# Two chunks of 256 tokens at once in the first layer behind the attention

## The chip, the cores and the metric

The kernel runs on one core of one Trainium2 chip. A core has a matrix engine (TensorE, PE in the profile, with its weight loads shown as PEld), VectorE (DVE), ScalarE (ACT), GpSimd (POOL) and SyncE (SP), which here issues all DMAs. Products go to eight PSUM banks of 2 KB for each of 128 partitions; everything else lies in SBUF. The metric is the device time of one execution in microseconds, as a median over several runs.

## The reference

An attention with a memory term feeds two feed-forward layers. All inputs are float32.

```
x = g * (phi(q) @ M_prev) / (phi(q) . z_prev) + (1 - g) * softmax(causal(q k^T / 8)) @ v   # 4 x 8 heads, 576 tokens, 64 wide
x = x as 2304 tokens x 512
h = x @ moe_w_in;   a = 0 where h <= -1, h where h >= 1, (h + 1)^2 / 4 between;   x = a @ moe_w_out
h = x @ moe2_w_in;  a = max(0.01 h, h);                                          out = a @ moe2_w_out
```

The weights are 512 x 2048 and 2048 x 512, and come as 64-bit floats that the kernel decodes itself.

## The kernel before

**Tiling.** The 2304 tokens are nine chunks of 256 (`TC`), held transposed: 128 partitions by four blocks of model width by 256 tokens. The 2048 hidden units are two halves (segments) of eight slots of 128. The first layer runs over the nine chunks with the first half, then over the nine chunks with the second, so it has eighteen numbered chunks, 0 to 17; the second layer has eighteen more, 18 to 35. A chunk of the first layer is eight steps, one for each slot.

**One step.** Each operand is split into a high and a low float32r part, and a product is high x high + high x low + low x high. `mm_h` (L551) makes 12 products of 256 columns into one bank (four blocks of model width, three each). ScalarE passes twice over the result (L565, L566), VectorE takes the minimum with the third form (L567), makes the high part (L569, a cast) and the low part (L571, a subtraction). Two steps later `mm_y` (L575) uses them in 12 products of 256 columns that accumulate, over the eight steps, into two banks: four output blocks of 256 columns, two in a bank. `finish` (L586) empties the two banks. In the first half ScalarE copies the sums (L593) and SP stores them to DRAM; in the second half VectorE adds what was stored before, brought back by `load_prev` (L540), and SP stores the result (L595, L597).

**Banks.** There are five banks called A, two called y and one called h. Behind the attention, the first products of a step take a bank A in turn, and the sums of even chunks go to the two y, those of odd chunks to h and one A (L716). So a chunk's sums and the next chunk's are in different banks.

**What sets the order.** Up to chunk 5 the first layer is woven into the attention, and a scheduler may move instructions. Behind it (L823) TensorE, ScalarE, VectorE and GpSimd run in the order in which the code is written; SP's queue is still placed by the scheduler. Beside the steps stand jobs, given by step number: fetching and decoding weight halves from 64-bit form (L118 to L135, five VectorE instructions and one of ScalarE) and splitting them into high and low parts (L200, L204). Their VectorE instructions are put between those of a step by `fill` (L194): before the cast, before the low part, and behind it. The load of the next chunk's x is issued in step 3, and its split (`high_x` on ScalarE, `low_x` on VectorE) in step 5.

**Buffers.** Tiles live in pools. The attention's pool is closed when the first weights of the second half need room, and a second pool opens over it. `g`, the high and the low part have two buffers each: the high part of step f is written where that of step f - 2 was, when its second products are done.

Of the kernel before, what the change touches and what calls it, by code (L numbers as in the profile page):

```python
# [20 lines left out]
TC = 256  # L21
# [9 lines left out]
again = {n for n, (s, c) in enumerate(CHUNKS) if any(SEGS[t][0] == SEGS[s][0] and d == c for t, d in CHUNKS[:n])}  # L31
NW, RAWB, SPB, EB, GB = 4, 3, 2, (2, 2, 2, 2, 1), 2
# [19 lines left out]
def attn_moe_moe_kernel(ctx, tc, q, k, v, m_prev, z_prev, beta, w1i, w1o, w2i, w2o, out):  # L52
# [92 lines left out]

    def load_raw(seg, f, x):
# [78 lines left out]
    def split_out(seg, p):  # L225


        if (seg, p) not in combos:
            combine(seg, p)
        b11, t1, b, t = combos.pop((seg, p))  # L230
        wa = wts.tile([128, 2, 512], F32R, tag=f"o{2 * p}", name="wa")
        wb = wts.tile([128, 2, 512], F32R, tag=f"o{2 * p + 1}", name="wb")
        ex = l2_pool().tile([128, 2, 768], F32R, tag=f"ex{p}", name="ex")
# [277 lines left out]
    def load_x(n):  # L511
        seg, c = CHUNKS[n]
        layer = SEGS[seg][0]
        xf = ffn.tile([128, 4, TC], F32, tag="xf", bufs=1, name="xf")
# [25 lines left out]
    def load_prev(n):  # L540

        seg, c = CHUNKS[n]
        if SEGS[seg][0] == 0:
            pp = ffn.tile([128, 1024], F32, tag="xf", bufs=1, name="xf")
        else:
            pp = l2_pool().tile([128, 1024], F32, tag="pp", name="pp")
# [4 lines left out]
    def mm_h(n, f):  # L551
        seg, c = CHUNKS[n]
        w = slots[f, 0]
        xh, xl = xin[n]
        hp = psum()[:, 0:TC] if attended else ps.tile([128, TC], F32, tag="h", bufs=HB, name="h")
        for ct in range(4):
            wh, wl = w[:, 0, 128 * ct:128 * ct + 128], w[:, 1, 128 * ct:128 * ct + 128]
            nc.tensor.matmul(hp, wh, xh[:, ct], start=(ct == 0), stop=False)  # L558
            nc.tensor.matmul(hp, wh, xl[:, ct], start=False, stop=False)  # L559
            nc.tensor.matmul(hp, wl, xh[:, ct], start=False, stop=(ct == 3))  # L560
        g = ffn.tile([128, TC], F32, tag="g", bufs=2, name="g")
        gh = ffn.tile([128, TC], F32R, tag="gh", bufs=GB, name="gh")
        gl = ffn.tile([128, TC], F32R, tag="gl", bufs=GB, name="gl")
# [4 lines left out]
        fill()  # L568
        nc.vector.tensor_copy(gh, g)  # L569
        fill()  # L570
        nc.vector.tensor_tensor(gl, g, as_r(gh), ALU.subtract)  # L571
        fill()
        return gh, gl

    def mm_y(n, f, yp, gg):  # L575
        w = slots[f, 1]
        gh, gl = gg
        for et in range(4):
            wh, wl = w[:, 0, 128 * et:128 * et + 128], w[:, 1, 128 * et:128 * et + 128]
            o = yp[et // 2][:, et % 2]  # L580

            nc.tensor.matmul(o, wh, gh, start=(f == 0 and et % 2 == 0), stop=False)  # L582
            nc.tensor.matmul(o, wh, gl, start=False, stop=False)  # L583
            nc.tensor.matmul(o, wl, gh, start=False, stop=(f == NSLOT - 1 and et % 2 == 1))  # L584

    def finish(n, yp):  # L586
        c = CHUNKS[n][1]
        pp = prev.pop(n, None)
        for i in range(2):
# [7 lines left out]
            nc.sync.dma_start(out=dst, in_=ys.rearrange("p (b t) -> p b t", b=2))  # L597


    def mm_h2(n, p):  # L600
# [12 lines left out]
        g = l2_pool().tile([128, 8, 128], F32, tag="g2", bufs=2, name="g2")  # L613
# [6 lines left out]
        gh = l2_pool().tile([128, 7, 128], F32R, tag="gh2", bufs=2, name="gh2")  # L620
        gl = l2_pool().tile([128, 7, 128], F32R, tag="gl2", bufs=2, name="gl2")
# [14 lines left out]
    def finish2(n, yp):  # L636
        seg, c = CHUNKS[n]
        pp = prev.pop(n, None)
        s0 = l2_pool().tile([128, 2, 256], F32, tag="s0", name="s0")
        s1 = l2_pool().tile([128, 2, 256], F32, tag="s1", name="s1")  # L640
# [41 lines left out]
    for seg in range(1, N1):  # L682
        x0 = START[seg]
        order = sorted((x0 + f + (-7, -5)[x], f, x) for f in range(NSLOT) for x in range(2))
# [27 lines left out]
    def layer1_y():  # L712
        nonlocal yp
        n, f, gg = pend.pop(0)
        if f == 0:
            yp = [bank(t) for t in ("h" + "Ah"[HB - 1] if attended and n % 2 else "yy")]  # L716
        mm_y(n, f, yp, gg)
        if f == NSLOT - 1:
            finish(n, yp)

    def layer1_steps():
        load_x(0)
        low_x(0, high_x(0))
        for n, (seg, c) in enumerate(CHUNKS):
            if SEGS[seg][0] == 1:
                break
            for f in range(NSLOT):
                do_jobs(8 * n + f)
                pend.append((n, f, mm_h(n, f)))
                if f == (3 if attended else 5):  # L730
                    load_x(n + 1)
                if f == 5:
                    low_x(n + 1, high_x(n + 1))
                if f == 6 and n in again:
                    load_prev(n)
# [118 lines left out]
```

## Time and profile before

| | |
|---|---|
| median of 3 runs | 1116.9 us (1115.13 to 1118.41) |
| the profiled execution | 1113.12 us, span of the trace 1111.3 us |
| TensorE busy | 1060.2 us, 8520 products |
| VectorE, ScalarE busy | 851.4 us, 612.4 us |
| mean granted TensorE clock | 0.98 of full speed |

The profile is one execution. A busy time is the union of an engine's instructions; products are pipelined, so their mean length (283 ns for 256 columns) is longer than the distance between their starts, and the distance is what counts. The time before an instruction in which its engine was idle is listed with what released it. The attention fills the first 430 us together with chunks 0 to 5 of the first layer; chunks 6 to 17 lie between 432 and 715 us, and the second layer behind them.

### The profile page before, as it was taken

To read this page: it belongs to the slowest core of one execution; us is meant where nothing else is said; L and a number is where in the kernel's file an instruction comes from. 1 tells how busy PE (TensorE), PEld (TensorE's weight loads), DVE (VectorE), ACT (ScalarE), POOL (GpSimd) and SP (SyncE) were. 2 spreads that over 40 slices of the span, in tenths; PEclk is the share of its full clock that TensorE was granted. 3 is DMA by queue.
4 is the path that set the end of the run, shared out by engine and by line. 5 is a ranking of instruction groups with operands and counts; after the bars stand their busy time and mean duration, and the time that the engine had idled before them with its cause. 6 is when DMAs were issued, how large, how long until landed. Compare 5 with 4: busy or idle time off the path is not lost.

```text
span 1111.3 us, 22273 instructions
## 1 busy us (share of the span) xinstructions
PE 1060.2 (95%) x8520; PEld 1002.1 (90%) x8520; DVE 851.4 (77%) x2244; ACT 612.4 (55%) x1379; POOL 28.9 (3%) x28
## 2 busy tenths in 40 slices
PE   5877899999999999999999999999999999999997
PEld 4655777888889889999999999999999999999997
DVE  6698899876777666985776777898887899657655
ACT  6898787666666664464333334554444465334332
POOL 0000000000000000000000000000000001112111
PEclk9888999999999999999999999999999999999999
DMA  6465545442334223531343333223222111311311
GB/s 145 115 166 150 161 129 160 121 117 68 88 79 120 65 58 93 168 100 56 96 152 115 116 117 121 86 77 133 95 96 96 58 39 49 104 58 65 103 44 58
DMA packets 122170, 112.08 MB, mean 101 GB/s; under 512 B 67280, under 2 KB 100048, under 8 KB 122064
## 3 DMA queue, kind: packets, MB, share of 16 engines
q1 hardware_dynamic: 122064, 110.66, 33.8%
q8 instruction: 67, 1.10, 0.4%
q14 instruction: 39, 0.32, 0.1%
HBM read 77.60 MB, written 23.59 MB: 91 GB/s over the span
## 4 chain that ended last, share of the span: by engine, by line
PE 81%; DVE 9%; DMA 4%; ACT 3%; issue 1%; SPq 1%; DVEq 0%; ACTq 0%
PE A L612 6%; PE A L611 6%; PE A L610 6%; PE A L558 4%; PE A L560 4%; PE A L559 4%; PE y L582 4%; PE y L583 4%; PE y L584 4%; PE y L634 3%; PE y L633 3%; PE y L632 3%; PE A L371 3%; PE A L423 2%; PE h L558 2%; PE h L559 2%
## 5 line engine op out<-in xcount | busy, mean ns | idle before, releaser
L612 PE MATMUL A<-xh,i 128*128 128x256 f32 x576 | 163.1, 283 | 0.1
L610 PE MATMUL A<-xh,i 128*128 128x256 f32 x576 | 163.0, 283 | 0.0
L611 PE MATMUL A<-xl,i 128*128 128x256 f32 x576 | 163.0, 283 | 0.0
L772 ACT ACTIVATE gh<-g 128x896 fp32r<-128x896 f32 x72 | 68.8, 955 | 125.0 <-PE A L633 74.2
L565 ACT ACTIVATE g<-A 128x256 f32<-128x256 f32 x98 | 37.6, 384 | 150.9 <-PE A L560 149.7
L751 DVE TENSOR_TENSOR gl<-g,gh 128x896 fp32r<-128x896 f32 x72 | 86.7, 1204 | 33.7 <-ACT gh L772 33.7
L558 PE MATMUL A<-xh,i 128*128 128x256 f32 x392 | 111.0, 283 | 0.0
L559 PE MATMUL A<-xl,i 128*128 128x256 f32 x392 | 110.9, 283 | 0.0
L560 PE MATMUL A<-xh,i 128*128 128x256 f32 x392 | 110.9, 283 | 0.0
L612 PEld LDWEIGHTS A<-xh,i 128*128 128x128 f32 x576 | 110.6, 192 | 0.3 <-DVE i L206 0.3
L610 PEld LDWEIGHTS A<-xh,i 128*128 128x128 f32 x576 | 110.6, 192 | 0.0
L611 PEld LDWEIGHTS A<-xl,i 128*128 128x128 f32 x576 | 110.6, 192 | 0.0
L583 PE MATMUL y<-gl,o 128*128 128x256 f32 x384 | 109.4, 288 | 0.0
L582 PE MATMUL y<-gh,o 128*128 128x256 f32 x384 | 107.4, 291 | 1.6 <-ACT ys L593 1.4
L584 PE MATMUL y<-gh,o 128*128 128x256 f32 x384 | 108.5, 285 | 0.0
L386 ACT ACTIVATE e<-e,mx 128x128 f32<-128x128 f32 (+2 forms) x144 | 84.2, 587 | 20.9 <-DVE mx L383 20.7
L383 DVE CUSTOM_DVE_ANT_0 e<-A,mask 128x384 f32<-128x384 f32 (+4 forms) x126 | 60.2, 481 | 45.0 <-PE A L371 43.8
L615 ACT ACTIVATE g<-A 128x512 f32<-128x512 f32 x72 | 42.8, 594 | 88.8 <-PE A L612 88.8
L567 DVE SCALAR_TENSOR_TENSOR g<-A,g 128x256 f32<-128x256 f32 x98 | 41.3, 422 | 55.6 <-ACT g L566 55.0
L558 PEld LDWEIGHTS A<-xh,i 128*128 128x128 f32 x392 | 75.2, 192 | 0.4 <-issue 0.4
L560 PEld LDWEIGHTS A<-xh,i 128*128 128x128 f32 x392 | 75.3, 192 | 0.0
L559 PEld LDWEIGHTS A<-xl,i 128*128 128x128 f32 x392 | 75.3, 192 | 0.0
(252 smaller groups left out, 3350.3 us busy)
## 6 DMA issues: line engine op xcount, KB each, us to landing
raw<-in_moe_w_in_dram SPq DMA_DIRECT2D x32, 512.0 KB, 3.8
raw<-in_moe_w_out_dram SPq DMA_DIRECT2D x32, 512.0 KB, 3.4
qk<-qk SPq DMA_DIRECT2D x64, 144.0 KB, 2.6
xf<-y_d SPq DMA_DIRECT2D x18, 512.0 KB, 4.2
xf<-x_d SPq DMA_DIRECT2D x12, 512.0 KB, 4.2
yp_d<-ys SPq DMA_DIRECT2D x18, 256.0 KB, 2.2
xf<-yp_d SPq DMA_DIRECT2D x9, 512.0 KB, 3.3
y_d<-ys SPq DMA_DIRECT2D x18, 256.0 KB, 2.2
```

The lines of the kernel that those rows point to most:

```text
L386: nc.scalar.activation(e[:, 0:w], e[:, 0:w], AF.Exp, bias=mx, scale=-1.0, accum_out=ls[:, h:h + 1])
L558: nc.tensor.matmul(hp, wh, xh[:, ct], start=(ct == 0), stop=False)
L559: nc.tensor.matmul(hp, wh, xl[:, ct], start=False, stop=False)
L560: nc.tensor.matmul(hp, wl, xh[:, ct], start=False, stop=(ct == 3))
L582: nc.tensor.matmul(o, wh, gh, start=(f == 0 and et % 2 == 0), stop=False)
L583: nc.tensor.matmul(o, wh, gl, start=False, stop=False)
L584: nc.tensor.matmul(o, wl, gh, start=False, stop=(f == NSLOT - 1 and et % 2 == 1))
L610: nc.tensor.matmul(o, wh, xh[:, ct], start=(s == 0 and ct == 0), stop=False)
L611: nc.tensor.matmul(o, wh, xl[:, ct], start=False, stop=False)
L612: nc.tensor.matmul(o, wl, xh[:, ct], start=False, stop=(s == 1 and ct == 3))
L751: nc.vector.tensor_tensor(gl, g[:, 1:8], as_r(gh), ALU.subtract)
L772: nc.scalar.activation(gg[1], gg[0][:, 1:8], AF.Copy)
```

## The change

Chunks 7 to 16 are taken in pairs: (7, 8), (9, 10) up to (15, 16), in the table `GROUPS`. A pair goes through eight steps as one chunk did. Its first products take two chunks' x as one moving operand of 2 x 256 columns and fill a whole bank; the passes on ScalarE and VectorE are 512 wide; its second products have 512 columns, and the sums take four banks, one for each output block: y, y, h and an A. `finish_pair` empties them in eight pieces of 256 columns and eight stores. Chunks 0 to 6 and 17 stay single.

The tiles of a pair (x before and after the split, `g`, high and low parts) lie in a pool `pairs` in the room of the attention; it is closed when the second layer's tiles need room, which now have a pool of their own behind it (`l2_room`). The sums that are brought back in the second half take the two buffers that x is loaded into. The jobs that split the second half's weights are given by 2f steps instead of f, and start 12 steps ahead of the second half instead of 7. Jobs of both step numbers of a pair run ahead of its step.

```diff
+GROUPS = [(n,) for n in range(7)] + [(n, n + 1) for n in range(7, 17, 2)] + [(17,)]
...
+    def split_x(n):
+        xh = pair_pool().tile([128, 2, 4, TC], F32R, tag="xh2", bufs=2, name="xh")
+        xl = pair_pool().tile([128, 2, 4, TC], F32R, tag="xl2", bufs=2, name="xl")
+        for i in range(2):
+            nc.scalar.activation(xh[:, i], xin[n + i], AF.Copy)
+            nc.vector.tensor_tensor(xl[:, i], xin[n + i], as_r(xh[:, i]), ALU.subtract)
+        xin[n] = (xh, xl)
...
-    def mm_h(n, f):
+    def mm_h(n, f, pair=False):
...
+        if pair:
+            hp = psum()
+            hx, xh, xl = hp.rearrange("p (i t) -> p i t", i=2), xh.rearrange("p i a t -> p a i t"), xl.rearrange("p i a t -> p a i t")
...
+            nc.tensor.matmul(hx, wh, xh[:, ct], start=(ct == 0), stop=False)
+            nc.tensor.matmul(hx, wh, xl[:, ct], start=False, stop=False)
+            nc.tensor.matmul(hx, wl, xh[:, ct], start=False, stop=(ct == 3))
+        if pair:
+            g = pair_pool().tile([128, 2 * TC], F32, tag="g", bufs=2, name="g")
+            gh = pair_pool().tile([128, 2 * TC], F32R, tag="gh", bufs=GB, name="gh")
+            gl = pair_pool().tile([128, 2 * TC], F32R, tag="gl", bufs=GB, name="gl")
...
-        fill()
+        fill(1 + pair)
...
+            if pair:
+                o, first, last = yp[et].rearrange("p i t -> p (i t)"), True, True
...
+    def finish_pair(n, yp):
+        for et in range(4):
+            if et < 3:
+                ys = (ffn if et < 2 else pair_pool()).tile([128, 2, TC], F32, tag="ys", bufs=2 - et // 2, name="ys")
+                ys = [ys[:, i] for i in range(2)]
+            else:
+                ys = [ffn.tile([128, TC], F32, tag="g", bufs=2, name="g") for i in range(2)]
+            for i in range(2):
+                c = CHUNKS[n + i][1]
+                if n in prev:
+                    nc.vector.tensor_tensor(ys[i], yp[et][:, i], prev[n + i][:, TC * et:TC * et + TC], ALU.add)
+                else:
+                    nc.scalar.activation(ys[i], yp[et][:, i], AF.Copy)
+                nc.sync.dma_start(out=(y_d if n in prev else yp_d)[c][:, et], in_=ys[i])
...
-        order = sorted((x0 + f + (-7, -5)[x], f, x) for f in range(NSLOT) for x in range(2))
+        order = sorted((x0 - 12 + 2 * f + 4 * x, f, x) for f in range(NSLOT) for x in range(2))
...
-            yp = [bank(t) for t in ("h" + "Ah"[HB - 1] if attended and n % 2 else "yy")]
-        mm_y(n, f, yp, gg)
+            tags = "yyhA" if pair else "hA" if attended and n % 2 else "yy"
+            yp = [bank(t) for t in tags]
+        mm_y(n, f, yp, gg, pair)
...
+        for group, after in zip(GROUPS, GROUPS[1:] + [(18,)]):
+            n, m, pair = group[0], after[0], len(group) == 2
             for f in range(NSLOT):
-                do_jobs(8 * n + f)
-                pend.append((n, f, mm_h(n, f)))
-                if f == (3 if attended else 5):
-                    load_x(n + 1)
+                for x in group:
+                    do_jobs(8 * n + len(group) * f + x - n)
+                pend.append((group, f, mm_h(n, f, pair)))
+                if len(after) == 2 and f in (2, 3):
+                    load_x(m + f - 2, True)
```

The line numbers of the changed kernel differ: L594 to L596 are the first products (L558 to L560 before), L626 to L628 the second ones (L582 to L584), L608, L610 and L612 VectorE's chain (L567, L569, L571), L125 to L137 the decode (L123 to L135) and L654 the adds of `finish_pair`.

On TensorE, from the last first product of a step to the end of its second products (`i` and `o` are weight tiles, `xh` and `gh` high parts, `gl` low ones), the order before is, in step 2 of chunk 7:

```order
L560 MATMUL A<-xh,i_1132 128x256
L582 MATMUL h<-gh,o_949 128x256
L583 MATMUL h<-gl,o_949 128x256
L584 MATMUL h<-gh,o_949 128x256
L582 MATMUL h<-gh,o_949 128x256
L583 MATMUL h<-gl,o_949 128x256
L584 MATMUL h<-gh,o_949 128x256
L582 MATMUL A<-gh,o_949 128x256
L583 MATMUL A<-gl,o_949 128x256
L584 MATMUL A<-gh,o_949 128x256
L582 MATMUL A<-gh,o_949 128x256
```

and now, in step 2 of pair (7, 8):

```order
L596 MATMUL A<-xh,i_1132 128x512
L626 MATMUL y<-gh,o_949 128x512
L627 MATMUL y<-gl,o_949 128x512
L628 MATMUL y<-gh,o_949 128x512
L626 MATMUL y<-gh,o_949 128x512
L627 MATMUL y<-gl,o_949 128x512
L628 MATMUL y<-gh,o_949 128x512
L626 MATMUL h<-gh,o_949 128x512
L627 MATMUL h<-gl,o_949 128x512
L628 MATMUL h<-gh,o_949 128x512
L626 MATMUL A<-gh,o_949 128x512
L627 MATMUL A<-gl,o_949 128x512
```

The banks h and A took two output blocks each; now y, y, h and A take one each, with twice the columns, and each row stands for two of before.

On VectorE, where one chunk's sums are emptied, the order before is, for chunk 11 (a decode in the step ahead, then the chain of step 1, and the two adds):

```order
L567 SCALAR_TENSOR_TENSOR g<-A,g 128x256
L127 SCALAR_TENSOR_TENSOR da<-w32b,da 128x512
L569 CAST gh<-g 128x256
L130 TENSOR_SCALAR dr<-da 128x512
L571 TENSOR_TENSOR gl<-g,gh 128x256
L132 SCALAR_TENSOR_TENSOR dr<-raw,dr 128x512
L135 TENSOR_TENSOR w32b<-da,dr 128x512
L567 SCALAR_TENSOR_TENSOR g<-A,g 128x256
L569 CAST gh<-g 128x256
L571 TENSOR_TENSOR gl<-g,gh 128x256
L595 TENSOR_TENSOR ys<-h,xf 128x512
L595 TENSOR_TENSOR ys<-A,xf 128x512
```

and now, for pair (11, 12), in step 1 of pair (13, 14):

```order
L125 TENSOR_SCALAR da<-raw 128x512
L608 SCALAR_TENSOR_TENSOR g<-A,g 128x512
L129 SCALAR_TENSOR_TENSOR da<-w32b,da 128x512
L132 TENSOR_SCALAR dr<-da 128x512
L610 CAST gh<-g 128x512
L134 SCALAR_TENSOR_TENSOR dr<-raw,dr 128x512
L137 TENSOR_TENSOR w32b<-da,dr 128x512
L612 TENSOR_TENSOR gl<-g,gh 128x512
L654 TENSOR_TENSOR ys<-y,xf 128x256 x4
L654 TENSOR_TENSOR ys<-h,xf 128x256 x2
L654 TENSOR_TENSOR g<-A,xf 128x256 x2
```

The decode, whose step number 106 lies in that pair step, stands in the same chain as the adds, and the adds have become eight of 256 columns from four banks.

## Rows read from the trace of the kernel before

**Rows 1.** The page: span, TensorE's busy time, shares of the chain that ended last.
```profile
span 1111.3 us, 22273 instructions
...
PE 1060.2 (95%) x8520; PEld 1002.1 (90%) x8520; DVE 851.4 (77%) x2244; ACT 612.4 (55%) x1379; POOL 28.9 (3%) x28
...
PE 81%; DVE 9%; DMA 4%; ACT 3%; issue 1%; SPq 1%; DVEq 0%; ACTq 0%
```

**Rows 2.** Windows of chunks 6, 7, 15 and 17; the columns are in the first line.
```profile
core 0: us, PE busy (x) PEld busy (x) DVE busy (x) ACT busy (x) POOL busy (x), PEclk, DMA share, GB/s
436.20:455.30 19.10, 19.10 (x161) 19.10 (x160) 18.25 (x43) 9.89 (x21) 0.00 (x0) 1.00 0.50 155
455.30:478.40 23.10, 23.10 (x195) 23.10 (x194) 22.35 (x53) 11.60 (x25) 0.00 (x0) 1.00 0.55 170
...
639.60:662.70 23.10, 23.10 (x195) 23.10 (x194) 16.46 (x40) 8.68 (x20) 0.00 (x0) 1.00 0.39 129
...
685.70:708.60 22.90, 22.90 (x193) 22.90 (x192) 18.11 (x44) 12.61 (x29) 0.00 (x0) 1.00 0.26 81
```

**Rows 3.** Timeline of TensorE, step 5 of chunk 7: start, length, engine, line, operation, count.
```profile
469.72 0.28 PE L558 MATMUL A<-xh,i 128*128 128x256 f32 x1
...
471.16 0.28 PE L582 MATMUL h<-gh,o 128*128 128x256 f32 x1
...
472.60 0.28 PE L558 MATMUL A<-xh,i 128*128 128x256 f32 x1
```

**Rows 4.** Timeline of TensorE, two 512-column products among 256-column ones.
```profile
391.32 0.28 PE L559 MATMUL h<-xl,i 128*128 128x256 f32 x1
391.44 0.62 PE L371 MATMUL A<-qk 128*128 128x512 f32 x2
391.90 0.28 PE L560 MATMUL h<-xh,i 128*128 128x256 f32 x1
```

**Rows 5.** Timeline of VectorE, end of chunk 6 and start of chunk 7.
```profile
451.33 1.22 DVE L537 TENSOR_TENSOR xl<-xf,xh 128x1024 fp32r<-128x1024 f32 x1
...
454.13 0.42 DVE L123 TENSOR_SCALAR da<-raw 128x512 int32<-128x512 int32 x1
454.46 0.28 DVE L569 CAST gh<-g 128x256 fp32r<-128x256 f32 x1
454.67 0.68 DVE L127 SCALAR_TENSOR_TENSOR da<-w32b,da 128x512 int32<-128x512 int32 x1
455.27 0.42 DVE L571 TENSOR_TENSOR gl<-g,gh 128x256 fp32r<-128x256 f32 x1
455.61 0.42 DVE L130 TENSOR_SCALAR dr<-da 128x512 int32<-128x512 int32 x1
456.06 0.69 DVE L132 SCALAR_TENSOR_TENSOR dr<-raw,dr 128x512 f32<-128x512 uint32 x1
456.78 0.69 DVE L135 TENSOR_TENSOR w32b<-da,dr 128x512 f32<-128x512 f32 x1
457.39 0.42 DVE L567 SCALAR_TENSOR_TENSOR g<-A,g 128x256 f32<-128x256 f32 x1
...
458.24 0.43 DVE L571 TENSOR_TENSOR gl<-g,gh 128x256 fp32r<-128x256 f32 x1
458.58 0.42 DVE L567 SCALAR_TENSOR_TENSOR g<-A,g 128x256 f32<-128x256 f32 x1
```

**Rows 6.** Timeline of ScalarE, step 7 of chunk 6.
```profile
454.08 0.39 ACT L565 ACTIVATE g<-A 128x256 f32<-128x256 f32 x1 [1.48 <-PE A L560]
454.50 0.42 ACT L566 ACTIVATE g<-g 128x256 f32<-128x256 f32 x1
```

**Rows 7.** Groups by line and shape, 436 to 715 us: an eviction on ScalarE.
```profile
L615 ACT ACTIVATE g<-A 128x512 f32<-128x512 f32 x1 | 0.6, 597 | 2.7 <-PE A L612 2.7
```

**Rows 8.** Waits of all engines, 436 to 715 us: waiter, releaser, total, times, longest.
```profile
DVE gh L569 <- PE A L584: 1.4, 9, 0.2
```

**Rows 9.** The page: DMA issues, KB each and median us to landing.
```profile
y_d<-ys SPq DMA_DIRECT2D x18, 256.0 KB, 2.2
```

More of the change, by code (lines that the diff above doesn't have):

```diff
@@ L144, in l2_pool, with pair_pool, l2_room @@
         return phase[0]
+    pairs, room = [], []
+    def pair_pool():
+        if not pairs:
+            l2_pool()
+            pool = tc.tile_pool(name="pairs", bufs=1, reuse_waits="tile")
+            pairs.extend((pool, pool.__enter__()))
+        return pairs[1]
+    def l2_room():
+        if not room:
+            pairs[0].__exit__(None, None, None)
+            room.append(ctx.enter_context(tc.tile_pool(name="l2b", bufs=1, reuse_waits="tile")))
+        return room[0]
     def load_raw(seg, f, x):
@@ L232, in split_out @@
         wb = wts.tile([128, 2, 512], F32R, tag=f"o{2 * p + 1}", name="wb")
-        ex = l2_pool().tile([128, 2, 768], F32R, tag=f"ex{p}", name="ex")
+        ex = l2_room().tile([128, 2, 768], F32R, tag=f"ex{p}", name="ex")
         split(wa[:, :, 0:256], b11)
@@ L509, in attn_moe_moe_kernel, with load_x @@
     xin, prev = {}, {}
-    def load_x(n):
+    def load_x(n, pair=False):
         seg, c = CHUNKS[n]
         layer = SEGS[seg][0]
-        xf = ffn.tile([128, 4, TC], F32, tag="xf", bufs=1, name="xf")
+        if pair:
+            xf = pair_pool().tile([128, 4, TC], F32, tag="xf2", bufs=2, name="xf")
+        else:
+            xf = ffn.tile([128, 4, TC], F32, tag="xf", bufs=1, name="xf")
         if layer == 0:
@@ L538, in low_x, with load_prev @@
         xin[n] = (xh, xl)
-    def load_prev(n):
+    def split_x(n):
[5 more added lines that the diff above has]
+        xin[n] = (xh, xl)
+    def load_prev(n, pair=False):
         seg, c = CHUNKS[n]
-        if SEGS[seg][0] == 0:
+        if pair:
+            pp = pair_pool().tile([128, 1024], F32, tag="xf2", bufs=2, name="xf")
+        elif SEGS[seg][0] == 0:
             pp = ffn.tile([128, 1024], F32, tag="xf", bufs=1, name="xf")
         else:
-            pp = l2_pool().tile([128, 1024], F32, tag="pp", name="pp")
+            pp = l2_room().tile([128, 1024], F32, tag="pp", name="pp")
         src = yp_d[c] if SEGS[seg][0] == 0 else op_d[c]
@@ L579, in mm_y @@
             wh, wl = w[:, 0, 128 * et:128 * et + 128], w[:, 1, 128 * et:128 * et + 128]
-            o = yp[et // 2][:, et % 2]
-            nc.tensor.matmul(o, wh, gh, start=(f == 0 and et % 2 == 0), stop=False)
+            if pair:
+                o, first, last = yp[et].rearrange("p i t -> p (i t)"), True, True
+            else:
+                o, first, last = yp[et // 2][:, et % 2], et % 2 == 0, et % 2 == 1
+            nc.tensor.matmul(o, wh, gh, start=(f == 0 and first), stop=False)
             nc.tensor.matmul(o, wh, gl, start=False, stop=False)
-            nc.tensor.matmul(o, wl, gh, start=False, stop=(f == NSLOT - 1 and et % 2 == 1))
+            nc.tensor.matmul(o, wl, gh, start=False, stop=(f == NSLOT - 1 and last))
     def finish(n, yp):
@@ L713, in layer1_y @@
         nonlocal yp
-        n, f, gg = pend.pop(0)
+        group, f, gg = pend.pop(0)
+        n, pair = group[0], len(group) == 2
         if f == 0:
-            yp = [bank(t) for t in ("h" + "Ah"[HB - 1] if attended and n % 2 else "yy")]
-        mm_y(n, f, yp, gg)
+            tags = "yyhA" if pair else "hA" if attended and n % 2 else "yy"
+            yp = [bank(t) for t in tags]
+        mm_y(n, f, yp, gg, pair)
         if f == NSLOT - 1:
-            finish(n, yp)
+            (finish_pair if pair else finish)(n, yp)
     def layer1_steps():
@@ L723, in layer1_steps @@
         low_x(0, high_x(0))
-        for n, (seg, c) in enumerate(CHUNKS):
-            if SEGS[seg][0] == 1:
-                break
+        for group, after in zip(GROUPS, GROUPS[1:] + [(18,)]):
+            n, m, pair = group[0], after[0], len(group) == 2
             for f in range(NSLOT):
-                do_jobs(8 * n + f)
-                pend.append((n, f, mm_h(n, f)))
-                if f == (3 if attended else 5):
-                    load_x(n + 1)
-                if f == 5:
-                    low_x(n + 1, high_x(n + 1))
-                if f == 6 and n in again:
-                    load_prev(n)
+                for x in group:
[3 more added lines that the diff above has]
+                    load_x(m + f - 2, True)
+                if len(after) == 1 and f == (3 if attended else 5):
+                    load_x(m)
+                if f == 5:
+                    if len(after) == 2:
+                        split_x(m)
+                    else:
+                        low_x(m, high_x(m))
+                if f == 6:
+                    for x in group:
+                        if x in again:
+                            load_prev(x, pair)
                 if len(pend) > LAG:
```

33 lines of the change are left out of this document (17 added, 16 removed).

## The prediction

> **What bounds the kernel now.** I read the page first: TensorE is busy for 1060.2 of 1111.3 us and holds 81% of the chain that ended last [rows 1]. Then a table of windows, one for each chunk of the changed stage. In chunks 6 to 17 TensorE is busy for the whole of each window at a granted clock of 1.00, which is 2.4 GHz, while VectorE is nearly full in chunks 6 and 7 (18.25 of 19.10 us, 22.35 of 23.10) and has room later (16.46 of 23.10) [rows 2]. So in this stage TensorE's own instructions set the time, and the reader is to see two things: what one product costs, and how near VectorE comes to being late. For the first I read the timeline of TensorE. One step (12 first products, 12 second ones) runs from 469.72 to 472.60 us, which is 24 starts in 2.88 us, or 120 ns for 256 columns [rows 3]. At 2.4 GHz the columns alone take 106.7 ns, so 13.3 ns of each product are not columns. A chunk is 8 such steps, 23.04 us, and chunk 7 begins at 469.72 - 5 x 2.88 = 455.32 us.
>
> **The change: fewer, wider products.** Ten chunks (7 to 16) are 10 x 8 x 24 = 1920 products of 256 columns; they become 960 of 512. The trace of before has 512-column products of the same type in the attention. Two of them, between streams of 256-column ones, start at 391.44, and the next instruction starts at 391.90: 460 ns, 230 ns each [rows 4]. Against 2 x 120 = 240 ns this is 10 ns for each new product: 960 x 10 = 9.6 us. The bounds: if the 13.3 ns are a fixed cost of a product, 512 columns take 226.7 ns and the gain is 960 x 13.3 = 12.8 us; if they go with the columns, 240 ns and nothing. I take 230, which is measured, and which comes with a weight load of its own, as here.
>
> The Trainium skill, "TensorE: Matmul & The Clock Gate", section "Back-to-back issue gap", gives the columns over 2.4 GHz plus 2.5 ns for a warm product. By that, 960 fewer products would save an estimated 2.4 us. The trace does not agree: the excess is 13.3 ns at 256 columns and 16.7 at 512, and the measurement decides.
>
> The moving operand of the first products is now two runs of 256 columns from two halves of a tile. No row shows such a form. If the seam cost as much as a second product saves, 480 x 10 = 4.8 us would go; if nothing, zero. Below zero nothing is to be had, since no column falls away. I take zero, the nearest row being an operand in one run [rows 4].
>
> **Evictions and splits.** For each pair step VectorE runs one chain of 512 instead of two of 256. Starts in the trace give: the instruction on the product's result 0.60 (as 454.67 to 455.27 for 512 columns), the cast 0.33 (the 512-column single-source instruction at 454.13 to 454.46), the subtraction 0.61 (456.78 to 457.39), sum 1.54; before it was 2 x (0.34 + 0.21 + 0.34) = 1.78, with the first taken as long as the subtraction [rows 5]. The gain of 0.2 us a step is off the path; it is cover. The weight decodes (0.33 + 0.60 + 0.45 + 0.72 + 0.61 = 2.71 us each) and the splits stay, and move to pair steps.
>
> **Where cover is thin, 1: the first pair.** In chunk 6 a second 1.22 us subtraction for x is added. VectorE was already late there: the result of step 7 was ready at 454.50 + 0.42 = 454.92 [rows 6], but it was taken up at 457.39, and its low part ended at 458.24 + 0.43 = 458.67 [rows 5]. TensorE needed it at 455.32 + 2.88 + 1.44 = 459.64. After the change it is ready at 459.9, but two wide first products (12 x 230 = 2.76 us) and one narrow set lie ahead of its use: 455.32 + 2.76 + 1.44 + 2.76 = 462.28. Behind it wait two decodes in step 0 and one in step 1. VectorE is free at 459.8, does step 0 (1.54 + 5.42) until 466.8, and step 1's low part by 466.8 + 1.54 + 2.71 = 471.1 at the latest. TensorE wants that at 455.32 + 2 x 1.44 + 5 x 2.76 = 472.0. So 0.9 us is left, and more later, since a step lasts 5.52 us. Cost zero, cover 0.9 us; a decode more at this place would turn it into a wait of 1.8 us.
>
> **Where cover is thin, 2: the hand-over of the accumulators.** Before, even and odd chunks used different banks. Now a pair fills four (y, y, h, A), and the next pair needs the same y, y and h. Put time 0 where TensorE begins the last second products of the old pair; they end at 2.76, the new pair's first products of step 2 at 5.52, and there bank 1 must be empty, bank 2 at 6.21, bank 3 at 6.90. ScalarE's two passes on step 1's result end near 1.5 (0.60 for 512 columns [rows 7]; the second, not shown at 512, 0.42 + 0.21 from the 256-column rows [rows 6]). VectorE's first instruction ends at 2.15. Its cast must wait until the old pair's last product is out, because it overwrites the high part of step 7: it starts at 2.53 and takes 0.39 (0.62 for two, less 0.23 between their starts [rows 4]), so 2.92. Such waits stand in the trace already, 9 of them, 0.2 us at most [rows 8]. Cast and subtraction run until 3.9. Behind them in VectorE's queue are the eight adds of 256 columns, 0.34 apart [rows 5]: bank 1 is free at 3.9 + 0.34 + 0.42 = 4.7, banks 2 and 3 each 0.68 later. Margin 0.8 us. Of the four hand-overs between pairs, the first has no adds but copies on ScalarE (some 0.39 each [rows 6]), which wait for no cast and end earlier. Two are as worked out. In the third, pair 11 to pair 13, a decode falls on step 1: two of its instructions go ahead of the cast and two ahead of the subtraction, which moves the adds to 5.5 and bank 1 to 6.3. TensorE then waits 0.8 us. Into chunk 17 the narrow chain ends near 2, and bank 3 is free at about 4.1 where it is wanted at 4.2; there also step 2's tile is one that the old pair's last sums are stored from, so ScalarE waits for a store (2.2 us after its issue [rows 9]). That brings step 2's low part to where TensorE wants it; I take 0.2 us.
>
> **DMA.** The eight stores of a pair carry the same bytes in runs of 1 KB; nothing but that tile waits for them. SP now issues a second load of x ahead of the raw weights queued behind it; what these lose comes out of the 0.9 us above, and nothing is charged.
>
> **Sum.** -9.6 + 0.8 + 0.2 = -8.6 us. The profiled execution took 1113.12 us (1.8 us around its span of 1111.3) and would come to 1104.5. The median of the three runs is 1116.9, so 3.8 us above it; a run like the median comes to **1108.3 us**. For this kernel 0.3%, or 3.4 us, is what a measurement can tell from no change.
>
> **Rivals.**
> - *Wholly fixed cost.* 226.7 ns per product: -12.8 + 1.0, 1105.1 us. For it: 13.3 ns at 256 columns is what a fixed cost would look like. Against it: the measured 230. Chance 0.15.
> - *The excess goes with the columns, or the seam costs.* Gain 0 to 4.8 us less the 1.0 of waits: 1113.1 to 1117.9, no change. For it: 512 columns do show a larger excess than 256. Against it: that growth is 3.4 ns, not 13.3. The skill's 2.5 ns would land here as well, at an estimated 1115.5. Chance 0.09.
> - *VectorE is late at every hand-over.* TensorE, which has waited for nothing here, waits in front of the new pair's accumulation. If VectorE is late by L, two hand-overs cost L - 0.8 and one L + 0.8; at L = 3.4 us (somewhat over one decode) that eats the gain, and beyond it the kernel is slower. A whole pair step late, 5.52 us, is 2 x 4.7 + 6.3 = 15.7, so 1116.9 - 9.6 + 15.7 = 1123. For it: one set of banks, no spare, VectorE full in chunks 6 and 7. Against it: these hand-overs lie in chunks 11 to 15, where VectorE has 6.6 us of room a chunk [rows 2]. Slower 0.07; a smaller lateness that leaves no measurable change 0.06.
> - *That the change does not do what it says* is out: the order has 960 rows fewer on TensorE, and the wide ones stand at their place.
>
> **How the numbers follow.** The forecast has 0.63, and its own range is 1106 to 1111.5 (2.3 us more gain, towards the fixed cost, or 3.2 us of further waits). With the rivals: faster by more than 0.3% 0.63 + 0.15 + 0.01 of the seam case = 0.79; the same 0.14; slower 0.07. The range of 8 in 10 reaches from 1104, the full fixed cost, to 1114, half of the way into the no-change cases.
>
> **What would show it.** In the trace after: starts of the wide products 230 ns apart (227, 240 would be the rivals); a pair step of 5.52 us and a pair of 44.2 us instead of 46.1; 960 fewer products; TensorE idle about 0.8 us ahead of the second products of pair 13's step 0 and nowhere else over 0.3 us; VectorE still behind in pair 7 without TensorE waiting. The forecast is wrong if the pitch is 235 or more, or if TensorE stands for more than 1 us at two or more hand-overs.

## The result, and the profile after

| | before | after |
|---|---|---|
| median (lowest to highest) of 4 runs, us | 1116.24 (1115.13 to 1118.41) | 1102.71 (1101.77 to 1106.52) |
| profiled execution, us | 1113.12 | 1103.35 |
| its span, us | 1111.3 | 1101.4 |
| last product of the attention to first of layer 2, us | 280.69 | 269.65 |
| from there to the end of the span, us | 402.58 | 402.21 |

The ratio is 0.9883, with an interval of 0.9854 to 0.9912: faster, and by more than was forecast (1108.3 us). The measured time lies below the lower end of the range, 1104.

The page of the kernel after, the same three lines as [rows 1]: TensorE has 960 instructions fewer, and its share of the chain is what it was.
```profile
span 1101.4 us, 20167 instructions
...
PE 1051.8 (95%) x7560; PEld 955.8 (87%) x7560; DVE 838.2 (76%) x2140; ACT 597.6 (54%) x1303; POOL 28.9 (3%) x28
...
PE 81%; DVE 8%; ACT 4%; DMA 4%; issue 1%; SPq 1%; DVEq 0%; ACTq 0%
```

Windows of the kernel after, one for each stage: chunk 6, the pairs 7, 9, 11, 13 and 15, and chunk 17 (columns as in [rows 2]).
```profile
437.70:456.80 19.10, 19.10 (x161) 19.10 (x160) 18.25 (x41) 10.73 (x22) 0.00 (x0) 1.00 0.54 172
456.80:500.30 43.50, 43.50 (x205) 36.49 (x204) 41.72 (x77) 22.59 (x38) 0.00 (x0) 1.00 0.47 148
500.30:543.80 43.50, 43.50 (x193) 36.02 (x193) 25.36 (x43) 17.71 (x33) 0.00 (x0) 1.00 0.23 73
543.80:587.40 43.60, 43.60 (x194) 36.08 (x194) 30.97 (x58) 14.00 (x22) 0.00 (x0) 1.00 0.39 121
587.40:631.90 44.50, 43.78 (x193) 35.90 (x192) 29.82 (x56) 14.55 (x23) 0.00 (x0) 1.00 0.41 130
631.90:675.40 43.50, 43.50 (x199) 36.24 (x198) 29.86 (x57) 13.83 (x23) 0.00 (x0) 1.00 0.34 109
675.40:699.00 23.60, 23.45 (x176) 22.27 (x175) 18.62 (x47) 11.66 (x27) 0.00 (x0) 1.00 0.25 80
```
A pair takes 43.5 us where two chunks took 2 x 23.04 = 46.08. TensorE is idle in two windows only, those of pair 13 and of chunk 17 (ends of products are modelled, so a short gap shows as less idle time than it is long), and the clock is full throughout, as before. In pair 7 VectorE is busy for 41.72 of 43.50 us, and TensorE waits for nothing there.

The timeline of TensorE where pair 7 begins, which answers to [rows 3, 4]: narrow products, then twelve wide ones, then narrow ones again.
```profile
456.69 0.28 PE L628 MATMUL y<-gh,o 128*128 128x256 f32 x1
456.81 0.40 PE L594 MATMUL A<-xh,i 128*128 128x512 f32 x1
457.05 0.40 PE L595 MATMUL A<-xl,i 128*128 128x512 f32 x1
457.28 0.39 PE L596 MATMUL A<-xh,i 128*128 128x512 f32 x1
...
459.11 0.39 PE L595 MATMUL A<-xl,i 128*128 128x512 f32 x1
459.34 0.39 PE L596 MATMUL A<-xh,i 128*128 128x512 f32 x1
459.56 0.28 PE L626 MATMUL y<-gh,o 128*128 128x256 f32 x1
```
The first starts are 0.24 and 0.23 us apart, the last 0.23 and 0.22. The timeline rounds to hundredths, so a pitch is better read over many starts. One wide step of pair 7, 24 products, from its first product to the first of the next step, in the same view:
```profile
481.52 0.39 PE L594 MATMUL A<-xh,i 128*128 128x512 f32 x1
...
484.24 0.39 PE L626 MATMUL y<-gh,o 128*128 128x512 f32 x1
```
Twelve products are 2.72 us, 226.7 ns each. The unrounded records say the same: behind 923 of the 960 wide products the next one starts 226 or 227 ns later. At 2.4 GHz 512 columns are 213.3 ns, so 13.3 ns are left, exactly what was left at 256 columns. The Trainium skill, "TensorE: Matmul & The Clock Gate", section "Back-to-back issue gap", would have an estimated 213.3 + 2.5 = 215.8 ns for an isolated product and some 131 for a sustained stream; neither is what this stream shows.

### Where the time went

The stage that was changed is 11.04 us shorter. That is 960 x 13.33 = 12.80 us for the width, less 1.76 us of further gaps between products. I found these by subtracting (columns over 2.4 GHz + 13.33 ns) from each distance between two starts. Before, the sum over the stage was 0.10 us; after, it is 1.86: 0.96 us at the hand-over to pair 13, 0.31 and 0.34 us in chunk 17, some 0.1 us for changes of width, and the 0.10 that was there before.

Layer 2 is 0.37 us shorter, of which 0.27 come from a wait 14 us into it, for a weight split on VectorE, that has shrunk. The attention ahead of the stage ended 1.50 us later in this execution (429.57 against 428.07 us). The three parts, -11.04 - 0.37 + 1.50 = -9.91, make up the difference of the spans, 9.9.

That 1.50 us is within the scatter of that part. In the profiled executions of this study with an unaltered attention, its end lies anywhere between 424.76 and 432.40 us, and the stage and layer 2 behind it repeat within 0.05 us for the same kernel. Up to there TensorE, VectorE, ScalarE and GpSimd run the same instructions in the same order in both kernels. So the medians carry that scatter, and the trace gives what the change does from there on: -11.04 - 0.37 = -11.4 us.

Scatter about the same mean would fall to either side, though, and it doesn't. In all seven timed sets of runs of changed kernels (this one and those below), the median lies further below the median of before than the two traces have it for the stage and layer 2, by 0.8 to 2.1 us, and so it does where the products are narrow again (1.4 us). So some 1 us more seems to go ahead of the stage. It doesn't look like the width of the products, but what it is stays open: the sets share runs of before, and the stage of before is known from one trace.

### The profile page after: what moved, and what is told of

Same layout as the page of the kernel before. It is cut to its first block, busy times and chain, and to the rows that moved or that the text cites. A ratio compares the mean times of both kernels' runs of the same rounds, so it can differ in the third digit from the quotient of the medians.

```text
span 1101.4 us, 20167 instructions
## 1 busy us (share of the span) xinstructions
PE 1051.8 (95%) x7560; PEld 955.8 (87%) x7560; DVE 838.2 (76%) x2140; ACT 597.6 (54%) x1303; POOL 28.9 (3%) x28
## 4 chain that ended last, share of the span: by engine, by line
PE 81%; DVE 8%; ACT 4%; DMA 4%; issue 1%; SPq 1%; DVEq 0%; ACTq 0%
PE A L672 6%; PE A L670 6%; PE A L671 6%; PE A L594 4%; PE A L596 4%; PE A L595 4%; PE y L626 4%; PE y L627 4%; PE y L628 4%; PE y L694 3%; PE y L693 3%; PE y L692 3%; PE A L389 3%; PE h L594 2%; PE A L441 2%; PE A L474 2%
## 5 line engine op out<-in xcount | busy, mean ns | idle before, releaser
L672 PE MATMUL A<-xh,i 128*128 128x256 f32 x576 | 163.1, 283 | 0.0
L670 PE MATMUL A<-xh,i 128*128 128x256 f32 x576 | 163.0, 283 | 0.0
L671 PE MATMUL A<-xl,i 128*128 128x256 f32 x576 | 163.0, 283 | 0.0
L672 PEld LDWEIGHTS A<-xh,i 128*128 128x128 f32 x576 | 110.6, 192 | 0.0
L670 PEld LDWEIGHTS A<-xh,i 128*128 128x128 f32 x576 | 110.6, 192 | 0.0
L671 PEld LDWEIGHTS A<-xl,i 128*128 128x128 f32 x576 | 110.6, 192 | 0.0
L627 PE MATMUL y<-gl,o 128*128 128x256 f32 (+1 forms) x304 | 95.8, 319 | 0.0
L626 PE MATMUL y<-gh,o 128*128 128x256 f32 (+1 forms) x304 | 93.6, 322 | 1.7 <-DVE ys L654 0.7
L628 PE MATMUL y<-gh,o 128*128 128x256 f32 (+1 forms) x304 | 94.9, 315 | 0.0
L594 PE MATMUL A<-xh,i 128*128 128x512 f32 (+1 forms) x232 | 82.7, 357 | 0.0
L595 PE MATMUL A<-xl,i 128*128 128x512 f32 (+1 forms) x232 | 82.6, 356 | 0.0
L596 PE MATMUL A<-xh,i 128*128 128x512 f32 (+1 forms) x232 | 82.6, 356 | 0.0
L608 DVE SCALAR_TENSOR_TENSOR g<-A,g 128x512 f32<-128x512 f32 (+1 forms) x58 | 35.1, 605 | 56.0 <-ACT g L607 56.0
L389 PE MATMUL A<-qk 128*128 128x384 f32 (+3 forms) x224 | 62.0, 361 | 10.6 <-DMA qk<-qk 6.4
L626 PEld LDWEIGHTS y<-gh,o 128*128 128x128 f32 x304 | 56.3, 192 | 6.4 <-ACT ys L637 1.1
```

The source lines that it names most:

```text
L389: nc.tensor.matmul(s[:, 0:n], qk[:, h, 128 * i:128 * i + 128], qk[:, h, 512 + S * x:512 + S * x + n], start=(x == 0), stop=(x == 1))
L594: nc.tensor.matmul(hx, wh, xh[:, ct], start=(ct == 0), stop=False)
L595: nc.tensor.matmul(hx, wh, xl[:, ct], start=False, stop=False)
L596: nc.tensor.matmul(hx, wl, xh[:, ct], start=False, stop=(ct == 3))
L626: nc.tensor.matmul(o, wh, gh, start=(f == 0 and first), stop=False)
L670: nc.tensor.matmul(o, wh, xh[:, ct], start=(s == 0 and ct == 0), stop=False)
```

## Experiments

All are edits of the kernel after. Kernels that were timed are compared with the kernel before on the same chip. The "further gaps" are those of the section above.

### The same kernel again

> The changed kernel once more, beside the kernel before on one chip, to size the gain. Theory A (each product costs its columns at 2.4 GHz plus a fixed 13.3 ns): the 960 removed products are worth 12.8 us, the waits and the changes of width seen in its trace cost 1.8 us, so 11.0 us less than before, some 1105 us if before takes 1116. Theory B (the gain of 13.5 us by the first medians is real and holds something beside TensorE's products): 13 us or more. In the trace both expect 226.7 ns between wide products, the first five of a wide run at 229 to 236, and one wait of 1 us at the sums of pair 13.

No edit. Measured: 1103.23 us (1098.79 to 1109.70, 6 runs) against 1115.83 of before (23 runs), ratio 0.9902 [0.9875, 0.9930]. The stage took 269.66 us, layer 2 402.26. Both intervals hold the -11.4 us of the trace (0.9898 of 1116); the 12.6 us between these medians lie between the two theories, and the interval rules out neither. The span of this execution, 1096.7 us, is 4.7 shorter than that of the first profile, and 4.81 us of it is an earlier end of the attention (424.76 us).

### Pairs, but every product 256 columns wide

> Pairs, banks, 512-wide passes on ScalarE and VectorE, loads, stores and jobs stay as changed; each 512-column product is issued as two of 256. Theory A: the products go back to 120 ns, ten chunks to 230.4 us, so 12 us more than the changed kernel and no gain against before (within 2 us of it). Theory B, that the pairing itself (fewer and longer instructions on VectorE and ScalarE, banks, room) brought part of the gain: 3 us or more below before.

```
             if pair:
+                for a, b, k in ((wh, xh, 0), (wh, xl, 1), (wl, xh, 2)):
+                    for i in range(2):
+                        nc.tensor.matmul(hx[:, i], a, b[:, ct, i], ...)
...
             if pair:
+                for k, (a, b) in enumerate(((wh, gh), (wh, gl), (wl, gh))):
+                    for i in range(2):
+                        nc.tensor.matmul(yp[et][:, i], a, b[:, TC * i:TC * i + TC], ...)
```

Measured: 1115.13 us, ratio 0.9991 [0.9977, 1.0005]; the stage took 281.75 us. Everything else of the change is still there (pairs, tiles, four banks, chains of 512 on VectorE and ScalarE), and nothing of the gain of the stage is left. The groups of TensorE in the changed stage of this kernel (line, engine, operation and shapes | busy us, mean ns | idle before, releaser):
```profile
L597 PE MATMUL A<-xh,i 128*128 128x256 f32 x640 | 109.4, 283 | 0.0
...
L630 PE MATMUL y<-gh,o 128*128 128x256 f32 x320 | 58.1, 283 | 0.3 <-DVE ys L664 0.3
```
So the gain of the stage is the width of the products alone, and with it their number and that of the weight loads, which can't be told apart here. The pairing costs a little by itself: its further gaps are 1.16 us, 0.57 of them at the hand-over to pair 13. There the wait is 0.39 us shorter than with wide products, which fits a step in front of it of 5.76 us instead of 5.44. Layer 2 takes 402.24 us here too, so its 0.3 us come with the pairing and not with the width.

### Only the first products 256 columns wide

> Only the first products of a pair step are issued as 24 of 256 columns; the second ones stay 12 of 512, so each of the 40 pair steps changes the width twice. Theory A: 480 products more than in the changed kernel, +6.4 us, with the wide ones at 226.7 ns. Theory C (a wide product behind narrow ones costs 230 ns or more for the first five, and the narrow one behind wide ones is 7 ns short): 21 ns more a step, 0.8 us in all, so +7.2 us, a pair step of 5.62 us. Theory of the prediction (230 ns for every wide product): the 12 wide ones take 2.76 us in each step, +7.8 us with the same narrow ones.

The edit is the first half of the one above. Measured: 1112.12 us, ratio 0.9973 [0.9958, 0.9987]; the stage took 278.25 us, 8.6 more than with all products wide. Of these, 480 x 13.33 = 6.4 us are the width. The further gaps are 4.07 us, 2.2 more than after. Of that, 0.8 us lie in the 40 steps in which the width now changes and changes back, 20 ns a step. The distance between starts by place in the run, median over the 40 steps, from the records of this trace:

```
512-column product after 256-column ones, place 1 to 8:  233 236 228 233 231 226 227 227 ns
256-column product after 512-column ones, place 1 to 4:  114 119 120 120 ns
```

So a run of wide products begins with five that are 1 to 9 ns late, and gives 6 to 7 ns back where it ends. The rest of the further gaps are waits, and chunk 17 has the larger ones; because of them the 8.6 us are more than any of the three theories had. The wide products are back at 226 to 227 ns from the sixth on, which speaks against 230 for each. The timeline of TensorE in chunk 17, step 2, of this kernel (behind the instruction: idle time, releaser):
```profile
698.41 0.28 PE L602 MATMUL A<-xh,i 128*128 128x256 f32 x1
699.66 0.38 PE L632 MATMUL h<-gh,o 128*128 128x256 f32 x1 [0.97 <-DVE gh L616]
700.60 0.39 PE L633 MATMUL h<-gl,o 128*128 128x256 f32 x1 [0.55 <-DVE gl L618]
```
Here TensorE stands for 1.13 + 0.81 us where the kernel after stands for 0.34. What shifts the store and VectorE's queue against TensorE in this kernel I didn't follow further; the next experiment takes this wait away.

### Without the two waits

> The decode at step number 106 goes to 108, a pair step later, and the last pair's fourth sums are stored from a tile of the pair's pool, not from chunk 17's. If the wait of 1 us at the sums of pair 13 comes from the decode that stands ahead of the adds on VectorE, it goes, and none takes its place; if the single set of banks is the cause by itself, it stays at 0.5 us or more. If the two waits in chunk 17 (0.3 us each) come from the store out of its tile, they go. Both: 1.6 us less than the changed kernel, a TensorE with no wait over 0.1 us between chunk 6 and the second layer.

```
-HALVES = {N1: [82 + 7 * i // 2 for i in range(16)], ...
+HALVES = {N1: [108 if i == 7 else 82 + 7 * i // 2 for i in range(16)], ...
...
             else:
-                ys = [ffn.tile([128, TC], F32, tag="g", bufs=2, name="g") for i in range(2)]
+                if n == 15:
+                    ys = pair_pool().tile([128, 2 * TC], F32, tag="g", bufs=2, name="g")
+                    ys = [ys[:, TC * i:TC * i + TC] for i in range(2)]
+                else:
+                    ys = [ffn.tile([128, TC], F32, tag="g", bufs=2, name="g") for i in range(2)]
```

The decode that fell on the hand-over moves one step on, and the last pair stores its fourth sums from a tile that chunk 17 doesn't use. Measured: 1101.18 us (1099.69 to 1103.25), ratio 0.9869 [0.9848, 0.9890]; the stage took 268.29 us, 1.36 less than after. The wait in the kernel after, by TensorE and then by VectorE, at the start of pair 13's second products:
```profile
598.26 0.39 PE L596 MATMUL A<-xh,i 128*128 128x512 f32 x1
599.36 0.47 PE L626 MATMUL y<-gh,o 128*128 128x512 f32 x1 [0.72 <-DVE ys L654]
```
```profile
594.54 0.69 DVE L608 SCALAR_TENSOR_TENSOR g<-A,g 128x512 f32<-128x512 f32 x1 [2.52 <-ACT g L607]
595.14 0.68 DVE L129 SCALAR_TENSOR_TENSOR da<-w32b,da 128x512 int32<-128x512 int32 x1
595.86 0.43 DVE L132 TENSOR_SCALAR dr<-da 128x512 int32<-128x512 int32 x1
596.20 0.42 DVE L610 CAST gh<-g 128x512 fp32r<-128x512 f32 x1
596.54 0.69 DVE L134 SCALAR_TENSOR_TENSOR dr<-raw,dr 128x512 f32<-128x512 uint32 x1
597.26 0.69 DVE L137 TENSOR_TENSOR w32b<-da,dr 128x512 f32<-128x512 f32 x1
597.87 0.69 DVE L612 TENSOR_TENSOR gl<-g,gh 128x512 fp32r<-128x512 f32 x1
598.47 1.41 DVE L654 TENSOR_TENSOR ys<-y,xf 128x256 f32<-128x256 f32 x4
```
Four instructions of a decode (L129 to L137) stand between the pair's own three (L608, L610, L612), and the adds that empty the bank begin only at 598.47. The same place without the decode, timeline of TensorE in this experiment:
```profile
596.24 0.39 PE L596 MATMUL A<-xh,i 128*128 128x512 f32 x1
596.46 0.39 PE L626 MATMUL y<-gh,o 128*128 128x512 f32 x1
596.69 0.39 PE L627 MATMUL y<-gl,o 128*128 128x512 f32 x1
```
No wait, and none came up in its place: the step that the decode moved to has room. Of the two waits in chunk 17 the second is gone as well, and the list of waits shows why. After, ScalarE stands for a store and TensorE's weight load for the subtraction behind it (waits of all engines, 437 to 699 us: waiter, releaser, total, times, longest):
```profile
DVE gh L610 <- PE A L628: 8.0, 11, 0.7
ACT g L606 <- DMA y_d<-g: 5.4, 1, 5.4
...
PE y L626 <- DVE ys L654: 0.7, 1, 0.7
...
PEld h L627 <- DVE gl L612: 0.3, 1, 0.3
```
In the experiment the same list has:
```profile
DVE gh L610 <- PE A L628: 8.1, 11, 0.7
...
PEld h L626 <- PE A L596: 0.3, 1, 0.3
```
The first wait in chunk 17 stays (0.31 us), so it isn't the store. The first line of each list is the cast that waits for the old pair's last product, 11 times instead of the 9 of [rows 8] and for longer; it didn't reach TensorE.

### A decode at each of the three hand-overs

> The decodes at step numbers 89 and 120 move to 90 and 122, so that step 1 of pairs 11, 13 and 15 each has one decode in VectorE's queue ahead of the adds that empty the accumulators. Theory A (the wait is the decode's 2.7 us less a margin): a wait of 1 us at each of the three hand-overs, where the changed kernel has one: 2.0 us more in the stage. Rival (the wait at pair 13 has another cause, such as the loads of the stored sums, or the single set of banks): one wait as before, and the two others under 0.3 us.

```
-HALVES = {N1: [82 + 7 * i // 2 for i in range(16)], ...
+HALVES = {N1: [{89: 90, 120: 122}.get(x, x) for x in (82 + 7 * i // 2 for i in range(16))], ...
```

One run, 1103.81 us; the stage took 271.72 us, 2.07 more than after. The waits of TensorE, and the window of pair 11, of this kernel:
```profile
PE y L626 <- DVE ys L654: 2.2, 3, 0.7
```
```profile
543.80:587.40 43.60, 42.88 (x189) 35.13 (x189) 31.60 (x59) 13.62 (x23) 0.00 (x0) 1.00 0.39 123
```
Three times the same wait: gaps of 0.96 us at 554, 599 and 643 us, and 0.72 us of idle time in pair 11's window, which had none after. Whether TensorE waits at a hand-over depends on whether a decode falls on the step in front of it. The free time on VectorE in the window, some 12 us, did not prevent it.

### First products in pieces of 128 columns

> The first products of a pair step are issued as 48 of 128 columns in place of 12 of 512, the second ones stay wide. Theory A, a fixed 13.3 ns for each product whatever its width: 66.7 ns each, 3.20 us for the 48 in place of 2.72, and the stage 40 x 0.48 = 19 us longer than in the changed kernel. Rival L, the weight load that each product brings sets a floor: 107 ns or more each, 5.1 us for the 48, and the stage some 97 us longer. Rival P, the excess shrinks with the width (57 ns between products of 128 columns, as in the attention's undisturbed pairs): 2.74 us, within 2 us of the changed kernel.

```
             if pair:
+                for a, b, k in ((wh, xh, 0), (wh, xl, 1), (wl, xh, 2)):
+                    for i in range(2):
+                        for j in (0, 128):
+                            nc.tensor.matmul(hx[:, i, j:j + 128], a, b[:, ct, i, j:j + 128], ...)
```

One run, 1210.73 us; the stage took 376.43, some 107 us more than after, nearest to the 97 of the rival with the weight load. The end of a step's first products on TensorE's timeline (the last number is the count of instructions in a row):
```profile
482.73 1.06 PE L598 MATMUL A<-xh,i 128*128 128x128 f32 x8
483.62 0.61 PE L598 MATMUL A<-xl,i 128*128 128x128 f32 x4
484.07 0.61 PE L598 MATMUL A<-xh,i 128*128 128x128 f32 x4
484.51 0.45 PE L633 MATMUL y<-gh,o 128*128 128x512 f32 x1
```
Sixteen products in 1.78 us are 111 ns each. The columns take 53.3 ns, and with 13.3 more it would be 66.7. So "columns plus 13.3 ns" holds at 256 and 512 columns and not at 128: there something else takes 111 ns for each product. A weight load stands with every product here; the Trainium skill, "TensorE: Matmul & The Clock Gate", section "LDWEIGHTS (loading the stationary operand)", gives one of 128 columns an estimated 106.7 ns (columns over 1.2). The 111 ns lie just above that, as they would if the load were the floor. But no run here has a product without its load, and the attention of the kernel before has eight transposes of 128 columns with eight weight loads of 128 columns, at a granted clock of 1.00:
```profile
193.60 0.80 PEld L293 LDWEIGHTS A<-ident_r,sp 128*128 128x128 f32 x8
193.70 0.84 PE L293 MATMUL A<-ident_r,sp 128*128 128x128 f32 x8
194.38 0.35 PE L583 MATMUL y<-gl,o 128*128 128x256 f32 x1
```
That is 0.68 us for eight, 85 ns each. So a product with such a load can follow another in less than 106.7 ns, at least in a transpose, and that the load sets the 111 ns isn't shown.

### Chunk 17's sums in other banks

> As the kernel with the moved decode and the other store tile, and chunk 17 gathers its sums in the two y banks, which the last pair empties first, in place of h and an A, which it empties last. If the 0.3 us that TensorE still waits at step 0 of chunk 17 is the emptying of h, it goes, and the stage is 0.3 us shorter; the second layer's first sums then follow chunk 17's in the same banks, and should that bind, as much or more is lost there. A time within 0.3% of the kernel with the moved decode either way.

The edit is that of "without the two waits", and in addition:
```
-            tags = "yyhA" if pair else "hA" if attended and n % 2 else "yy"
+            tags = "yyhA" if pair else "yy"
```
Measured: 1101.20 us (1100.03 to 1101.83), ratio 0.9869 [0.9845, 0.9893]; the stage took 267.99 us, 0.30 less than without this edit. The window of chunk 17 in this kernel:
```profile
675.40:699.00 23.60, 23.60 (x187) 23.03 (x186) 19.51 (x49) 12.40 (x27) 0.00 (x0) 1.00 0.24 81
```
TensorE is busy all the time, against 23.45 us after, and layer 2 loses nothing (402.25 us). So chunk 17's first wait was for bank h, which is the last but one that VectorE empties; the banks y are free earlier. In the times 0.3 us can't be seen.

### Without the two waits, again

> The kernel with the moved decode and the other store tile again, beside the one above: 12.8 us for the 960 products, less 0.3 us of waits and 0.1 us of changes of width, and some 0.4 us less in the second layer as in the changed kernel's trace: 12.8 us below before, 0.9885 of it.

The kernel without the two waits, once more, timed beside the one above: 1101.09 us (1098.12 to 1102.16), ratio 0.9867 [0.9843, 0.9890], stage 268.30 us. It repeats the first figures. This version beats both kernels: by its trace the kernel after by 1.36 us, in medians by some 2 us, which is inside the scatter of the runs.

### Longer runs of wide products in the attention

> The changed kernel, but in the attention each first score product of 512 columns is issued seven times into the same bank, so that a run of 512-column products there is 8 long instead of 2 (the repeats write the same values again; nothing is left out). Theory that the 230 ns of the two products read before was the start of a run: where 256-column products stand ahead of such a run, its first five starts are 229 to 236 ns apart, and from the sixth on they are 226 to 227 ns apart, as in the pairs. Rival that the attention's 512-column products have a longer pitch of their own: about 230 ns in every place of the run, or more. The time is longer by at most 28 x 6 x 0.227 = 38 us (28 such runs), less where TensorE waited there anyway; both say the same of it, about 1110 to 1141 us.

```
+for r in range(7 if n == 512 and x == 0 else 1):
     nc.tensor.matmul(s[:, 0:n], qk[:, h, 128 * i:128 * i + 128],
                      qk[:, h, 512 + S * x:512 + S * x + n],
-                     start=(x == 0), stop=(x == 1))
+                     start=(x == 0), stop=(x == 1 or n == 512 and r < 6))
```

One run, 1142.6 us, 1.6 above the upper bound that I gave. The bound had too few repeats in it: this trace has 192 products more than that of after, which is 32 x 6 and not 28 x 6, and with 32 the bound lies at some 1147. The wide products are those of the attention, like the two in [rows 4], now mostly eight or sixteen in a row. The distance from each to the next start, in ns, from the records of this trace:

```
at  98.30 us, after a product of 64 columns:  335 230 236 229 232 231 227 226 227 227 226 227 227 226 227 230
at 195.88 us, after products of 256 columns:  230 236 229 232 231 227 226 231
at 253.09 us, after products of 256 columns:  230 235 229 232 231 227 226 231
at 310.12 us, after products of 256 columns:  231 233 231 226 227 227 226 230
at 397.56 us, after products of 256 columns:  231 233 231 226 227 227 226 230
```
The first three to five are late, then the distance is 226 to 227, as in the pairs; the last, ahead of a product of another width, is 230 or 231. The attention's wide products have no pitch of their own. The two that I read had a pitch of 230 ns because there were two of them.

## Why the prediction was wrong

The direction and the mechanism were right: TensorE sets the time of this stage, fewer and wider products shorten it, and the waits came where they were placed. What failed is a term of the sum, the first and largest: **the 230 ns for a wide product**, and with it the 9.6 us. By step:

- **Pitch.** This is the step that failed. Forecast 230 ns, from two products in the attention [rows 4]; measured 226.7, so 12.8 us instead of 9.6. The rows were read correctly, but they show the beginning of a run, as the longer runs in the attention show directly; of the 960 products, 912 are one run. The rival "wholly fixed cost" had the right figure for 256 and 512 columns, and was put at 0.15 because a measured number seemed to speak against it. That 3.3 ns out of 230 might belong to the edge of a run, and not to each product of it, was not considered. Times 960 it is 3.2 us, three times all the waits that were worked out.
- **The seam in the moving operand.** Zero, as taken: the first products (operand in two runs of 256) and the second ones (in one run) both start 226 or 227 ns apart.
- **First pair.** Cover of 0.9 us, no wait: TensorE was busy for the whole of pair 7's window, with VectorE at 41.72 of 43.50 us. Right.
- **Hand-over to pair 13.** Forecast 0.8 us, measured 0.96 (0.88 for the wait itself, the rest in the next product), because of the decode and behind the very instructions that were named. Right in kind and nearly in size. The two other hand-overs had a margin of 0.8 by the working, and no wait; with a decode on them they wait for 0.96 each.
- **Chunk 17.** Forecast 0.2 us, measured 0.31 + 0.34. Both causes were named, the emptying of bank 3 (margin worked out as 0.1 us, missing by 0.31) and the store out of the tile; the first was counted as just in time and wasn't.
- **Changes of width.** Not in the sum. Some 20 ns each, five times: 0.1 us.
- **Layer 2.** Not in the sum: -0.37 us, most of it because VectorE is less late with a weight split near its start, which the kernel with narrow products shows as well.
- **The sum.** -12.8 + 0.96 + 0.65 + 0.1 - 0.37 = -11.5, and the trace has -11.4, against the forecast of -8.6. That is 2.8 us of the 5.6 between 1108.3 and 1102.71. Another 0.7 is that before had a median of 1116.24 in these runs and not 1116.9. The last 2.1 us are left: the medians differ by 13.5, the stage and layer 2 in the traces by 11.4. The interval of the ratio begins at a gain of 9.8 us, and the end of the attention scatters by 7.6 us between executions, so for one set of runs that is room enough. But the sign is the same in all seven sets, and the cause is open. Without these 2.1 us the time would have been 1104.8, just inside the range: the pitch made the forecast gain 3.2 us too small, and what carried the time past the end of the range is in part not explained.
- **The range.** Its lower end was set at the full fixed cost with the forecast's waits, 1105.1 rounded down to 1104. With nothing allowed for the scatter of a median of few runs, that end was too close to a rival that had a real chance.

## What to carry to other kernels

Where a sum multiplies one duration by a thousand, read that duration in the middle of a long stream of its kind; two instructions at an edge show the edge. If the trace has no such stream, use the difference that the narrow stream shows (13.3 ns beyond its columns at 256) as a value of equal standing, and set the range by it.

Before two accumulations share their banks, write down which instructions stand in the emptying engine's queue at the hand-over; one job that falls on that step costs what it pushes the emptying back by, less the margin (here 1.6 less 0.8 us by the working, 0.96 measured), however much room the engine has over the whole stage. Moving it by one step was worth 1 us for a changed number in a table.

## What the runs showed of the hardware

- With a weight load for each product, TensorE at 2.4 GHz started the products of this kernel 120.0 ns apart at 256 columns, 226.7 at 512 and 111 at 128. The first two are the columns plus 13.3 ns; the third is 57.8 ns above its columns, and what sets it isn't shown. Transposes of 128 columns in the attention, with a load each, started 85 ns apart.
- In the pairs, the first five wide products behind 256-column ones start 228 to 236 ns apart instead of 227, and the first narrow one behind them 113 or 114 instead of 120. The net cost was 20 ns for each change to and fro (40 steps). I don't know what makes it.
- The end of the attention part, in which TensorE waits for others, scattered by 7.6 us between executions; the changed stage and layer 2 repeated within 0.05 us for the same kernel. A comparison by stage tells apart differences of 0.3 us that the total time hides.
